# A fused attention and gMLP kernel on one core: a written-down job order, masks on TensorE, remainders in threes, and 19 DMA-transposed blocks

## The chip, the core and the metric

The kernel runs on one core of a Trainium2 chip. A core has five instruction queues: TensorE (PE, matmuls into the accumulator memory PSUM), VectorE (DVE), ScalarE (ACT), GpSimd (POOL) and SyncE (SP), which here does nothing but issue DMAs. The metric is the time of one execution on the device, in microseconds. PSUM has eight banks of 512 float32 values per partition.

## The reference

Input `x` has 2048 tokens of width 448. Two residual steps follow each other.

```
h  = x + Attn(layernorm(x))          # qkv = x @ wqkv, 16 heads of 28
h2 = h + Gmlp(layernorm(h))

Attn: token t looks at t, t-2, ..., t-14 (8 keys, those below 0 masked); softmax; @ wo
Gmlp: z = gelu(x @ w_in)             # 448 -> 1792, halves z1, z2
      g = w_sp @ layernorm(z2) + b_sp  # 2048 x 2048 over the tokens
      (z1 * g) @ w_out               # 896 -> 448
```

All inputs are bfloat16.

## The kernel before

**The attention.** The queries are cut into 18 blocks (`QN`: one of 128, nine of 112, eight of 114); a block's keys are its own tokens and the 14 before. Tokens are normalised in tiles of 128 (`stats`, `rstd_group`, `norm_transpose`) and transposed into `xhT`, on TensorE for the first eight tiles and by DMA after that. `qk_tile` makes 32 tiles of q or k of 512 tokens (four matmuls, one copy each), `v1_block` the values of a block. `scores` computes a block's 16 heads in 16 small matmuls on 28 of the 128 rows, ACT takes the exponential (L696), DVE multiplies it with a 0/1 mask (L700, three `Eslot` buffers), and `o_block` does 16 matmuls (L712) whose 29th column is the softmax's denominator; DVE divides (L720, L721). The result is transposed: by DMA where the block's length is a multiple of 16 (L726), else by TensorE with a copy out of PSUM (L729). `y_block` multiplies with `wo`, DVE adds the residual into `x_tm` (L743) and takes the statistics of the second layernorm.

**The gMLP.** The 448 input rows are three chunks of 128 and a remainder of 64. `packed` takes two accumulations at a time: six chunk matmuls of the first, the remainders of both (each pair on rows 0-63 and 64-127 of the array, L817), six chunk matmuls of the second (L811). There are 16 z2 blocks and 14 z1 tiles. Then 28 `g_tile`s (16 matmuls each, L874) alternate by token quarter with `wout_block`s (L898). In the last four blocks the residual enters PSUM through a matmul with the identity (L901); else DVE adds it.

**The order of the work.** Every operation is a job with a priority, a cost and the engines that can take it. `Sched.order` plays the jobs through once at build time: at each moment each free engine takes the ready job of the lowest priority number. What comes out is a fixed sequence for every queue, with semaphore waits between queues; on the chip an instruction that waits holds up all behind it on its queue. Banks 0-3 belong to the scores until the last block's scores have been placed. Warm-up matmuls (L573) have the priority 1e8, so they fill gaps. The mask is built by POOL and DVE at the start (L537 to L567, priorities -1000 and -300), the mixer's first matmuls depend on the load of the Gelu table (`r_gelu`), which depends on the last exponential.

## Time and profile before

| | |
|---|---|
| timed runs | 255.34, 255.38, 254.61 us (median 255.34) |
| the profiled execution | 254.57 us |
| its span, first to last instruction | 252.8 us |
| PE, DVE, ACT, POOL busy | 97%, 56%, 37%, 20% of the span |
| granted TensorE clock, mean | 0.993 |
| attention and lead-in / z2 and z1 / g and w_out | to about 82 / 82 to 131 / 131 to 249.8 us |

The time of an execution is longer than its span, since starting and ending it lie around the span. Views give an instruction's start from the span's start, its engine, its line and what it writes and reads. The chain of work that ended last is followed back from the last instruction: each piece was released by the one before, so what stands in it set the time. Matmuls overlap: the length of one (352 ns for 448 columns) is longer than the step from one to the next (189 ns), so costs on PE are read from starts.

### The profile page before, as it was taken

Reading aid. Unit: us, or ns where it says so; the run is one execution under the profiler, and the core shown is the slowest. Engines: PE = TensorE matmul, PEld = TensorE weight load, DVE = VectorE, ACT = ScalarE, POOL = GpSimd, SP = SyncE. Lnnn points to the kernel's source line nnn. Section 1 sums busy time; section 2 is a strip of 40 time slices with the busy share of each in tenths; the row PEclk is TensorE's granted clock in tenths of the full one; section 3 lists DMA queues with packets and bytes.
Section 4 is the critical chain, followed back from the end, with each engine's and each line's share of the span. In section 5 each row is a group of like instructions: output and inputs, shape, how many; then the busy total and the mean of one; then the engine's idle time right before and its main releaser. Section 6 shows DMA issues by size and latency. Waiting matters only on the chain.

```text
span 252.8 us, 4276 instructions
## 1 busy us (share of the span) xinstructions
PE 244.7 (97%) x1760; PEld 120.7 (48%) x1760; DVE 142.8 (56%) x303; ACT 93.3 (37%) x125; POOL 51.4 (20%) x85
## 2 busy tenths in 40 slices
PE   5799999999999999999999999999999999999995
PEld 1455555554555545444444444444444444444472
DVE  6798878789999888986203223423334332252240
ACT  2578787778599546666660000000000000000002
POOL 8305700002908480993000000000000000000000
PEclk9799999999999999999999999999999999999999
DMA  5931558956445591399999000020000100010002
GB/s 161 278 105 25 106 86 204 212 116 138 100 86 66 94 243 23 82 149 197 182 192 144 15 0 0 0 75 0 0 0 26 49 0 0 3 56 18 0 3 73
DMA packets 57060, 20.90 MB, mean 83 GB/s; under 512 B 50064, under 2 KB 56400, under 8 KB 57040
## 3 DMA queue, kind: packets, MB, share of 16 engines
q1 hardware_dynamic: 57040, 20.62, 39.2%
q8 instruction: 14, 0.23, 0.4%
q14 instruction: 6, 0.05, 0.1%
HBM read 6.60 MB, written 1.84 MB: 33 GB/s over the span
## 4 chain that ended last, share of the span: by engine, by line
PE 89%; ACT 4%; DVE 4%; DMA 1%; issue 0%
PE psum L874 38%; PE psum L811 15%; PE psum L657 10%; PE psum L898 8%; PE psum L670 5%; PE psum L740 3%; PE psum L817 3%; ACT regE L696 3%; PE psum L712 2%; PE psum L688 2%; ACT regW L582 1%; PE psum L639 1%; PE psum L573 1%; DVE ij L563 1%; DMA x_tm<-in_A_x_dram 1%; DVE x_tm L743 1%
## 5 line engine op out<-in xcount | busy, mean ns | idle before, releaser
L885 DVE TENSOR_TENSOR regE<-psum,regE 128x512 bf16<-128x512 f32 (+1 forms) x29 | 19.5, 674 | 76.3 <-PE psum L874 76.3
L874 PE MATMUL psum<-regW,regZ 128*128 128x512 bf16 (+1 forms) x240 | 48.9, 365 | 0.0
L874 PE MATMUL psum<-wspT_lo,regZ 128*128 128x512 bf16 x224 | 48.7, 379 | 0.0
L582 ACT ACTIVATE tring<-psum 128x448 bf16<-128x448 f32 x3 | 1.6, 545 | 116.4 <-PE psum L898 116.4
L874 PEld LDWEIGHTS psum<-regW,regZ 128*128 128x128 bf16 x240 | 23.4, 98 | 25.1
L874 PEld LDWEIGHTS psum<-wspT_lo,regZ 128*128 128x128 bf16 x224 | 21.9, 98 | 26.4
L657 PE MATMUL psum<-xhT,regZ 128*128 128x512 bf16 x128 | 31.1, 379 | 0.0
L696 ACT ACTIVATE regE<-psum 126x1792 bf16<-126x1792 f32 (+2 forms) x18 | 30.4, 1686 | 1.6 <-PE psum L688 1.5
L626 POOL TENSOR_SCALAR tring<-x_tm,ngm,rst 128x448 bf16<-128x448 bf16 (+1 forms) x32 | 24.5, 780 | 7.6 <-ACT rst L615 4.4
L898 PE MATMUL psum<-regE,regQ 128*128 128x448 bf16 x112 | 22.3, 352 | 0.0
L700 DVE TENSOR_TENSOR regE<-regE,maskb 126x1792 bf16<-126x1792 bf16 (+2 forms) x18 | 20.2, 1120 | 0.0
L811 PE MATMUL psum<-w_in,xhT 128*128 128x448 bf16 x96 | 19.5, 353 | 0.0
L593 DVE BATCH_NORM_STATS2 st<-x_tm 128x6 f32<-128x448 bf16 x32 | 18.6, 609 | 1.1 <-DMA x_tm<-in_A_x_dram 1.1
L811 PE MATMUL psum<-xhT,w_in 128*128 128x512 bf16 x84 | 19.0, 380 | 0.0
L670 PE MATMUL psum<-regW,xhT 128*128 128x448 bf16 (+1 forms) x72 | 17.2, 368 | 0.5 <-ACT rsy L613 0.5
L832 DVE BATCH_NORM_STATS2 st<-regZ 128x6 f32<-128x448 bf16 x32 | 17.5, 603 | 0.0
L657 PEld LDWEIGHTS psum<-xhT,regZ 128*128 128x128 bf16 x128 | 11.4, 97 | 11.9
L827 ACT ACTIVATE regZ<-psum 128x896 bf16<-128x896 f32 x16 | 14.0, 917 | 8.2 <-PE psum L817 6.1
L862 ACT ACTIVATE regQ<-psum 128x1024 bf16<-128x1024 f32 x14 | 13.7, 1023 | 8.4 <-PE psum L817 7.2
L582 ACT ACTIVATE regQ<-psum 128x512 bf16<-128x512 f32 x22 | 13.1, 597 | 8.8 <-PE psum L657 8.6
L898 PEld LDWEIGHTS psum<-regE,regQ 128*128 128x128 bf16 x112 | 11.0, 98 | 10.3
L582 ACT ACTIVATE regW<-psum 128x448 bf16<-128x448 f32 (+2 forms) x23 | 12.4, 551 | 7.3 <-PE psum L670 4.4
(70 smaller groups left out, 227.7 us busy)
## 6 DMA issues: line engine op xcount, KB each, us to landing
out_dram<-tring SPq DMA_DIRECT2D x16, 112.0 KB, 1.7
x_tm<-in_A_x_dram SPq DMA_DIRECT2D x3, 448.0 KB, 4.4
w_in<-in_B_w_in_dram SPq DMA_DIRECT2D x1, 1344.0 KB, 9.3
regE<-in_B_w_out_dram SPq DMA_DIRECT2D x1, 784.0 KB, 4.7
regW<-in_A_wqkv_dram SPq DMA_DIRECT2D x1, 672.0 KB, 5.7
regE<-in_B_b_sp_dram SPq DMA_DIRECT2D x1, 512.0 KB, 5.7
w_in<-in_B_w_in_dram SPq DMA_DIRECT2D x2, 224.0 KB, 9.3
regW<-in_A_wqkv_dram SPq DMA_DIRECT2D x1, 336.0 KB, 3.4
```

What stands on the lines that cost most here:

```text
L582: ways["act"] = (c, [lambda e: e.activation(dst(), src(), AF.Copy)])
L593: dve(prio, 0.62, lambda e: e.bn_stats(lnst[i][:, m, :], x_tm[:, m, :]), [r_x[m]], [r_stat[i][m]])
L626: job(prio, {"pool": (cp, [lambda e, c0=c0, c1=c1, s0=s0: e.tensor_scalar(tring[:, t.slot, c0:c1], x_tm[:, m, s0:s0 + c1 - c0], ngm[i][:, ...
L657: fns = [lambda e, c=c: e.matmul(bankcols(b, 512), wsrc[:, c, gg, :], xhT[:, c, col0:col0 + 512], start=(c == 0), stop=(c == NCH - 1)) for ...
L670: fns = [lambda e, c=c: e.matmul(bankcols(k, D)[0:nk], xhT[:, c, k0:k0 + nk], stg[:, c, 2 * D:3 * D], start=(c == 0), stop=(c == NCH - 1)) ...
L696: ej = job(prio + 1, {"act": (1.70, [lambda e: e.activation(Eheads(b), psum[0:nk, 0:2048].rearrange("p (h c) -> p h c", c=128)[:, :, 0:nq] ...
L700: dve(prio + 10, 1.12, lambda e: e.tensor_tensor(Eheads(b), Eheads(b), maskb[0:nk, mi:mi + 1, 0:nq].to_broadcast([nk, NHEAD, nq]), ALU.mul ...
L811: return [lambda e, i=i, c=c: e.matmul(out(i), lhs(i, c, slice(0, 128)), rhs(i, c, slice(0, 128)), start=(first and c == 0), stop=(not fir ...
L832: dve(prio + 2, 0.62, lambda e, i=i: e.bn_stats(st3[:, m, i, :], z2p[:, m, D * i:D * (i + 1)]), [r_z2p[m]], [r_stat[2][m]])
L874: fns = [lambda e, s=s: e.matmul(bankcols(k, n), z2p[:, s, fc * 128:(fc + 1) * 128], wsrc[:, s, coff:coff + n], start=(s == 0), stop=(s == ...
L885: dve(prio + 10, 0.70 * n / 512, lambda e: e.tensor_tensor(ub[:, u.slot, 0:n], bankcols(k, n), bb[:, t0:t0 + n], ALU.add), [k, r_bb], [u])
L898: fns = [lambda e, fc=fc: e.matmul(bankcols(k, D), z1p[:, fc, 128 * m:128 * m + 128], w_out[:, fc, :], start=(fc == 0 and not last), stop= ...
```

## The change

- **Order.** A list, `PLAN`, gives each of the 803 jobs its rank as its priority, and `ENGINE` ties 51 jobs to an engine. `Sched.order` still plays the jobs through, with other costs and latencies.
- **Blocks.** 19 blocks: 128, fourteen of 112, three of 96, one of 64. All are multiples of 16, so each output is transposed by DMA.
- **Masks.** For blocks 14 and 16 four matmuls of the identity with `maskn` (0 or -1e9) write PSUM first and the scores are added to that; DVE's multiplication is left out for these two.
- **Mask building.** The POOL work on it, and other fills, wait for the q/k weights; the DVE part has a later priority. The fill of `V1` with ones is cut to the one column that needs it.
- **Loads.** `x` block 1 is loaded ahead of the v weights.
- **q and k.** A `qk_tile` makes q and k together: eight matmuls into two banks and one copy of both.
- **Statistics.** For the first eight tiles of the second layernorm the final step (`bn_aggr`) is replaced by seven small POOL instructions (`aggregate`).
- **Remainders.** `packed` takes three accumulations, over z2 and z1 alike (30 in ten chains), and these depend on the last scores instead of the Gelu table.
- **The end.** The identity matmul is gone and DVE adds the residual in all blocks; block 15 is done in two halves of 224 columns, each with its own store.
- **Others.** 14 warm-up matmuls instead of 20; eight instead of nine w_sp blocks are loaded during the attention.

Counting jobs in the order in which they are made turns the list into names. TensorE begins: 7 warm-ups, transposes of tile 0, warm-up, tile 1, warm-up, v0, v1, warm-up, tile 2, warm-up, tile 3, warm-up, v2, q/k of tokens 0-511 (group 1, 0, 3), v3, warm-up, q/k group 2, warm-up, tiles 7, 5, scores 0, tiles 6, 4. The attention ends with: v17, scores 16, outputs 13, 15, y9, scores 17, output 16, y10, scores 18, first chunk of z2 block 0. The remainder jobs stand apart from each other, and three z1 tiles come ahead of z2 block 6. On DVE the order of the start is: statistics of tiles 0 and 1, normalise 0 and 1, statistics 3 and 2, copy of v0, normalise 2 and 3, first mask instruction, copy of tile 2, regrouping of a quarter of the q/k weights, the next mask instructions. SP issues: x0, x1, v weights, x2-3, the rest of v, q/k weights; later x transposes 8-11, w_sp 0, output 0, w_in, w_sp 1, x transposes 12-15, then outputs, w_sp blocks and transposes of h in turn.

```diff
-NWARM = 20
+NWARM = 14
+AGH = (0, 1)
+XPE = 2
+NLO = 8
+XONE = -99.7
+MKP = -100
+CHAIN = 3
+ADDMASK = (14, 16)
-QN = [128] + [112] * 9 + [NQ] * 8
+QN = [128] + [112] * 14 + [96] * 3 + [64]
+PLAN = (
+    15, 2, 21, 3, 1, 19, 0, 6, 4, 20, 44, 7, 18, 50, 5, 26, 57, 48, 8, 58, 16, 17, 54, 9, 59, 65, 60, 45, 61, 56,
...
-    LAT = {"pe": 0.20, "act": 0.10, "dve": 0.10, "pool": 0.15, "sp": 0.0}
+    LAT = {"pe": 0.12, "act": 0.06, "dve": 0.06, "pool": 0.08, "sp": 0.0}
...
-        load_x(-99, 1, 2)
-        load_x(-98.5, 2, 4)
+        load_x(XONE, 1, 2)
+        load_x(X23, 2, 4)
...
-        pool(2.2, lambda e: e.memset(V1, 1.0), writes=[r_Vones])
+        pool(0.2, lambda e: e.memset(V1[:, :, :, DH:DH + 1], 1.0), writes=[r_Vones])
+        pool(0.3, lambda e: e.iota(ij[:], [[1, 128]], base=0, channel_multiplier=1), r_stgqk[:1], [r_ij])
...
-        dve(-300, 0.2, lambda e: e.tensor_single_scalar(ij[:], ij[:], 1, ALU.bitwise_and), reads=[r_ij], writes=[r_ij])
+        dve(MKP, 0.2, lambda e: e.tensor_single_scalar(ij[:], ij[:], 1, ALU.bitwise_and), reads=[r_ij], writes=[r_ij])
...
+            dve(MKP + 1, 0.25, lambda e: e.tensor_scalar(maskn[:, 0, :], maskb[:, 0, 0:NQ], 1.0, MASKED, ALU.subtract, ALU.mult),
+                reads=[r_mask], writes=[r_maskn])
...
+        def aggregate(prio, i, lo, hi):
+            me, se, mo, so = (lnst[i][:, lo:hi, k] for k in (1, 2, 4, 5))
+            N, Y, T = (b_[i][:, lo:hi] for b_ in (ngm, rsy, rst))
...
+            p(lambda e: e.tensor_tensor(Y, me, mo, ALU.subtract), rs, [rc])
+            p(lambda e: e.tensor_tensor(N, me, mo, ALU.add), rs, r_ngm[i][lo:hi])
+            p(lambda e: e.tensor_tensor(Y, Y, Y, ALU.mult), [rc], [rc])
+            p(lambda e: e.tensor_tensor(T, se, so, ALU.add), rs, r_rstd[i][lo:hi])
+            p(lambda e: e.tensor_scalar(N, N, -0.5, 0.0, ALU.mult, ALU.add), r_ngm[i][lo:hi], r_ngm[i][lo:hi])
+            p(lambda e: e.tensor_scalar(T, T, 4.0 / D, 4.0 * EPS, ALU.mult, ALU.add), r_rstd[i][lo:hi], r_rstd[i][lo:hi])
+            p(lambda e: e.tensor_tensor(Y, Y, T, ALU.add), [rc] + r_rstd[i][lo:hi], [rc])
...
+        def qk_tile(prio, tc, gg):
...
+            b = Buf("qk%d_%d" % (tc, gg), p_bank, 2)
+            fns = [lambda e, i=i, w=w, c=c: e.matmul(bankcols(b, 512, i), w[:, c, gg, :], xhT[:, c, col0:col0 + 512],
+                                                     start=(c == 0), stop=(c == NCH - 1))
+                   for i, w in enumerate((wqp, wkp)) for c in range(NCH)]
+            copy(prio + 1, (1.22, 1.02), lambda: qkT[:, :, gg, col0:col0 + 512],
...
+            if b in ADDMASK:
+                add = [lambda e, hh=hh: e.matmul(
+                    psum[0:nk, hh * 512:hh * 512 + 512].rearrange("p (g c) -> p g c", c=128)[:, :, 0:nq],
+                    ident[0:nk, 0:nk], maskn[0:nk, 0:1, 0:nq].to_broadcast([nk, 4, nq]),
+                    start=True, stop=False, skip_group_check=True) for hh in range(4)]
+                fns = add + fns
...
-            one, two = jobs_
+            one, more = jobs_[0], jobs_[1:]
             turn = Buf("turn", p_turn)
+            job(one[0], {"pe": (cost(6, one), chunks(one, True))}, one[5], [one[1], turn])
+            fns = rest(one, True)
+            for p in more:
+                fns += rest(p, False)
...
+            parts = ((0, D // 2), (D // 2, D)) if m == NB - 1 else ((0, D),)
...
-                if last and n == 0:
-                    fns.insert(0, lambda e: e.matmul(bankcols(k, D), ident[:], x_tm[:, m, :], start=True, stop=False))
...
+        for rank, n in enumerate(PLAN):
+            sch.jobs[n].prio = rank
+        for eng, ns in ENGINE.items():
+            for n in ns:
+                sch.jobs[n].ways = {eng: sch.jobs[n].ways[eng]}
         sch.order()
```

More of the change, by code (lines that the diff above doesn't have):

```diff
@@ L242, in order @@
                     left[f] -= 1
-                    f.ready = max(f.ready, vis)
+                    f.ready = max(f.ready, end if set(f.ways) == {e} and not j.dma else vis)
                     if not left[f]:
@@ new lines, in wout_block @@
+            for h, (k, (c0, c1)) in enumerate(zip(ks, parts)):
+                t = Buf("out%d_%d" % (m, c0), p_tr)
+                dve(prio + 6 + h, 0.15 + 0.00106 * (c1 - c0), lambda e, k=k, t=t, c0=c0, c1=c1: e.tensor_tensor(
+                    tring[:, t.slot, c0:c1], bankcols(k, c1 - c0), x_tm[:, m, c0:c1], ALU.add), [k, r_x[m]], [t])
+                dma(prio + 7 + h, 112, lambda e, t=t, c0=c0, c1=c1: e.dma_start(OUT[128 * m:128 * m + 128, c0:c1], tring[:, t.slot, c0:c1]), [t], []).store = True
```

310 lines of the change are left out of this document (172 added, 138 removed), and 35 rows, old and new, of the table PLAN.

## The prediction

> **What bounds the kernel now.** I read the page first: TensorE (PE) is busy 97% of 252.8 us, so the question is which parts of that are work. The table of stretches answers it.
>
> ```profile
> 0.00:7.00 7.00, 3.52 (x8) 1.01 (x8) 4.83 (x9) 1.78 (x3) 6.36 (x20) 1.00 0.64 179
> 7.00:15.00 8.00, 7.40 (x40) 4.18 (x41) 6.00 (x20) 5.13 (x13) 1.70 (x5) 0.79 0.90 273
> ...
> 23.50:62.00 38.50, 38.50 (x508) 21.08 (x501) 31.85 (x57) 30.56 (x35) 7.38 (x9) 1.00 0.73 141
> 62.00:70.00 8.00, 7.97 (x86) 4.26 (x85) 7.81 (x18) 4.98 (x8) 6.18 (x9) 1.00 0.48 100
> 70.00:82.00 12.00, 11.01 (x180) 6.55 (x179) 11.65 (x24) 11.90 (x16) 5.70 (x8) 1.00 0.48 79
> ...
> 131.00:249.80 118.80, 118.77 (x581) 56.50 (x579) 39.08 (x70) 2.30 (x4) 0.00 (x0) 1.00 0.12 25
> ```
>
> Columns after the length: PE, weight loads, VectorE (DVE), ScalarE (ACT), GpSimd (POOL), the granted clock, DMA. From 15 us on PE is full except in 70 to 82, where ACT (11.90 of 12) and DVE (11.65) are full instead. The chain that ended last tells the same.
>
> ```profile
> 3.77 2.20 DVE ij L563
> ...
> 5.99 0.48 DVE pf L564
> ...
> 6.50 0.46 DVE pf L565
> ...
> 13.67 1.51 PE psum L670 x8
> 15.19 6.91 PE psum L657 x32
> ...
> 64.75 1.36 DVE regE L700
> ...
> 71.47 1.69 ACT regE L696
> 73.16 0.88 ACT regW L582 x2
> 74.04 1.58 ACT regE L696
> ```
>
> So three stretches do not belong to PE: the lead-in, where mask building (L563 to L565) holds DVE and with it the first normalisation; 62 to 68, where DVE owns the chain; and 71.5 to 81.3, where exponentials and PSUM copies on ACT do. All else is a stream of matmuls, and any matmul added or removed there moves the end by its own length.
>
> **The sum's base.** The profiled execution took 254.57 us, 1.77 more than its span and 0.3% under the median of the three timed runs (255.34; they lie between 254.61 and 255.38). Changes are added to 254.57. About 0.3% is also what a measurement of this kernel can tell from no change.
>
> **Lead-in.** Today block 0 is ready at 3.76 (its mean and variance), ACT's rsqrt ends at 4.33, but the normalisation runs only at 6.64, behind L563 (2.28 us) and its two followers; the first transposes start at 7.13, the first q/k tile at 15.02, by when PE has done four v blocks and four groups of transposes. In the changed order DVE goes from block 0's statistics to block 1's, then normalises: 3.76, plus 0.61 and 0.18 for block 1, plus 0.43, is about 5.0. What then gates the first q/k tile is the q/k weights (landed at 9.14 and 9.73), their regrouping (0.39 on DVE, 0.94 on ACT) and the copy of x block 3, which ACT has behind that regrouping: 9.73 + 0.94 + 0.60 is about 11.3; I take 11.4. The written order puts three v blocks before it, not four (0.80 each), so the gain is 15.02 - 11.4 - 0.80 = 2.8 us. Bounds: 3.4, if ACT's copy comes first; 1.6, if the first mask instruction, now just ahead of the copy of x block 2 on DVE, takes 2.28 again. Why did it take that?
>
> ```profile
> L563 DVE TENSOR_SCALAR ij<-ij 128x128 int32<-128x128 int32 x1 | 2.3, 2276 | 0.0
> L559 POOL MEMSET regW<- 128x2560 bf16 x1 | 2.2, 2231 | 0.0
> ```
>
> In the timeline L559 runs from 3.65 to 5.88 and L563 from 3.68 to 5.96: it ends as the memset does. The change shrinks the memset to one column in 32, and POOL's instructions beside the moved mask work take 0.24 to 0.39. [...]
>
> Warm-up matmuls go from 20 to 14. Two sit after the first q/k tiles (0.43 each), as two do today (22.60, 64.17): no difference. If the clock stays low longer (v blocks at 8.43 ran at half pace, 1.65 per four matmuls), that lies in the wait for the weights.
>
> **PE work.** Durations are starts of one job to the next, from the chain. Removed: eight groups of output transposes (L729, 0.20 to 0.21: 1.65) and four identity matmuls of the last four blocks (L901, 0.19: 0.76). Added: a nineteenth block, v 0.80 + scores 0.37 + output 0.39 = 1.56. Score jobs of 112 queries take 0.37, those of 114 take 0.31; eight of the latter go, eight x 0.06 = 0.48. The mask matmuls are four per block, of 448 and 384 columns. No row has this form; the nearest, full-height matmuls of 448 columns (L901), pace at 0.19, so 0.76 + 0.65 = 1.41; bounds 1.2 (in an open PE gap) and 1.8. Remainders (L817): today nine runs, each costing some 95 ns extra on the way in and again on the way out (a chunk before a remainder takes 285 or 311 instead of 189 or 216). The written order has ten separate runs of six: +0.2; bounds -0.9 (runs merge in pairs) and +0.2. In all -2.41 + 3.65, +1.2 us; bounds -0.1 and +1.6.
>
> **DVE, ACT and the stall.** From 71.45 to 82.50 PE did three v blocks, four transposes, five y blocks, three score and four output jobs, 9.4 us of work in 11.05: 1.7 waited. With 0.2 before 68.03, 1.9. The change takes from ACT eight copies of transposed output (0.56: -4.5) and about 1.9 in x copies, and adds a copy or so of net 1.2 (q/k copies go from 22 x 0.60 to 14 x 1.02, the price of a two-bank pass from L862), 0.9 of regrouping and 0.17 for one more exponential: about -4. From DVE it takes two masks (-2.2), eight aggregations (-1.4) and q/k copies (10 x 0.69 to two of at most 1.38: -4.1), and adds 0.85 (nineteenth block), 0.6 (v copy), 1.3 (x copies): about -5. Scores can also start some 5 us sooner, as first q/k tiles do, giving ACT that much more room, and the mixer's first matmuls wait only for the last scores. So I take the 1.9 as gone. What is late next is DVE: between the first q/k tile and the last scores it keeps some 60 us (15 masks 16, 17 divisions 15, 10 residual adds 6, 21 statistics 15, copies and normalisations 8) against 64 us of PE work, in a fixed order where each output job waits for its mask. A strict order on five queues will wait somewhere; the nearest row is today's own 1.9, and I take half of it, +1.0, bounds 0 and +4. Moving aggregation to POOL (seven instructions at 0.2 to 0.34, twice) puts about 2 us into the rsqrt of eight blocks; y and mixer work cover it. If that cover is gone, ACT's Ln waits with the next exponential behind it, 2 us each.
>
> **DMA.** Nine more output transposes ride SP's queue: 1.26 of queue time, 2.7 to landing, instead of 0.21 + 0.56 through PE and ACT. The y blocks that read them come some jobs later; cost nil while the queue keeps up (first rival). x block 1 goes ahead of the v weights by one 112 KB load: stgv landed at 4.65, xhT for the first v block is ready near 6, so it hides.
>
> **Tail.** The last block's copy took 0.62 after the last matmul; half a block (256 columns from PSUM took 0.42) saves 0.2. The extra store issue (0.33) lies under the second half's matmuls; bounds -0.3 and +0.3. After the last g tile (243.55) six matmuls (1.13) instead of seven cover its add and product on DVE, which ended 1.02 later: just hidden.
>
> **Sum:** -2.8 + 1.2 - 1.9 + 1.0 - 0.2 = -2.7; 254.57 - 2.7 = 251.9 us.
>
> **Rivals.** (1) SP's queue becomes the bound, slower. Between 22.8 and 82.0 it issued 33 transposes and three loads, 51.1 us busy of 59.2.
>
> ```profile
> 40.40 0.60 SPq L513 DMA_DIRECT2D w_in<-in_B_w_in_dram  x1
> 41.05 3.14 SPq L726 DMA_TRANSPOSE regW<-otm  x2
> 44.23 5.23 SPq L926 DMA_TRANSPOSE wspT_lo<-in_B_w_sp_dram  x1
> 49.50 2.57 SPq L726 DMA_TRANSPOSE regW<-otm  x2
> ```
>
> After the w_in load it stood for 5 us. Nine more transposes at 1.31 less one w_sp transpose are +10.2 against 8.1 free, in a window some 5 us shorter: 7 short. If none of it can go out later, outputs and normalised h land 7 late, y blocks and the mixer starve, and PE has nothing else: 251.9 - 1.0 + 7 = 258. It decides from about 3.7 us of such waiting on. Against it: four h transposes (5.1) are not needed until the mixer's second chain. Chance 0.15. (2) The stall only moves: DVE, near full, with two more long chains of POOL instructions beside it (a mask took 1.36 in the chain, 1.09 alone) keeps PE waiting as long as today or a little more: 1.9 to 2.6 in place of 1.0, 252.8 to 253.6, and with the lead-in's lower bound 254.8. [...] Chance 0.25. (3) The order fits so well that nothing new waits and the lead-in reaches 3.4: 251.9 - 1.0 - 0.6 - 0.3 = 250.0. Chance 0.15. The forecast itself, 250.6 to 253.2, has 0.45.
>
> **How the numbers follow.** The likeliest is 251.9. The range takes in the third rival with remainders merged (249.4) and reaches up to 255.6, which leaves out most of the first rival and a little below: under 2 in 10. Faster by over 0.3% means under 254.57: the forecast, the third rival and most of the second, 0.76; within 0.3%, the second's end and the start of the first, 0.09; slower 0.15.
>
> **What would show it.** First transposes near 5 and first q/k tile near 11.4; the first integer mask instruction well under 1 us; no transposes of outputs on PE; four 448-column matmuls of 0.19 ahead of two score jobs; ten remainder runs; mixer matmuls before the table load; PE's dense stretch from g to the last w_out shorter by 0.76 us; a last DVE piece near 0.4. The prediction is wrong if output jobs, y blocks or the first mixer chain wait more than 3 us in all, which the wait list would put down to DVE masks, to SP's transposes or to ACT's Ln, or if the first q/k tile starts after 13.

## The result, and the profile after

| | before | after |
|---|---|---|
| timed runs, median | 255.32 us (254.61 to 255.38, 4 runs) | 252.22 us (251.57 to 252.46, 4 runs) |
| profiled execution | 254.57 us | 252.46 us |
| its span | 252.8 us | 250.7 us |

The ratio is 0.9881, with a 95% interval of 0.9855 to 0.9907: the change makes the kernel 1.2% faster. The forecast was 251.9, in a range of 249.4 to 255.6. The sum was made for the profiled execution, where it foresaw 2.7 us less; there it is 2.11 less. Three of the four runs of the kernel before took about 255.3 here; in the experiments below it took over 255.0 in 16 of 48 runs and 254.4 to 254.9 in the rest. Against 254.6 the gain is 2.4 us, or 0.9%.

The table of stretches of the kernel after (columns as before: PE, weight loads, DVE, ACT, POOL, granted clock, DMA):

```profile
0.00:7.00 7.00, 4.55 (x18) 1.61 (x19) 4.22 (x10) 3.47 (x7) 2.51 (x13) 1.00 0.66 163
7.00:15.00 8.00, 6.79 (x36) 3.29 (x38) 5.74 (x17) 5.16 (x10) 4.11 (x11) 1.00 0.85 256
...
62.00:70.00 8.00, 7.84 (x110) 4.87 (x110) 7.46 (x14) 5.38 (x6) 6.06 (x8) 1.00 0.39 81
70.00:82.00 12.00, 11.71 (x189) 7.37 (x190) 10.27 (x22) 10.34 (x12) 5.55 (x15) 1.00 0.46 94
```

In 70 to 82 PE is busy for 11.71 us (11.01 before), while ACT fell from 11.90 to 10.34 and DVE from 11.65 to 10.27: neither is full there any more. (Some matmul records of this trace are missing, so PE's sums are a little low.) The chain that ended last, of the kernel after:

```profile
3.93 6.42 DMA regW<-in_A_wqkv_dram
...
10.43 0.95 ACT regZ L616
11.38 0.49 ACT xhT L663
11.88 0.14 issue
12.02 2.10 PE psum L762 x9
...
17.39 1.03 ACT regQ L663
18.42 0.05 issue
18.47 1.91 PE psum L762 x8
20.39 0.02 issue
20.41 1.03 ACT regQ L663
...
77.46 1.46 ACT regE L813
```

The mask building is gone from it. The lead-in is now a load (the q/k weights, landed at 10.35), their regrouping on ACT, the copy of x tile 3 behind that on the same engine, and the first q/k tile at 12.02. From there to the last matmul only three pieces do not belong to PE: two copies of q/k tiles (17.39 and 20.41) and one exponential (77.46).

To see where the 2.1 us come from, I cut each trace at the starts of certain matmuls. One v block (0.76) moved from before the first q/k tile to after it and is counted on the side where it was before.

| stretch | before | after | difference | foreseen |
|---|---|---|---|---|
| start to first q/k tile | 15.02 | 12.02 + 0.76 | -2.24 | -2.8 |
| first q/k tile to first g | 115.90 | 118.14 - 0.76 | +1.48 | +1.06 |
| first g to last matmul | 118.84 | 118.10 | -0.74 | -0.76 |
| last matmul to end of span | 3.06 | 2.47 | -0.59 | -0.2 |

Foreseen in the second row: PE work +1.2 without the identity matmuls' -0.76 that belong to the third row, the stall's -1.9 and the new waits' +1.0. So the attention as a whole became longer, and the gain lies at the two ends of the kernel. The experiments ask which parts of the change that is owed to.

### The profile page after: what moved, and what is told of

The parts are those of the page before. It is cut to its first block, busy times and chain, and to the rows that moved or that the text cites. A ratio compares the mean times of both kernels' runs of the same rounds, so it can differ in the third digit from the quotient of the medians.

```text
span 250.7 us, 4263 instructions
## 1 busy us (share of the span) xinstructions
PE 242.2 (97%) x1746; PEld 121.7 (49%) x1769; DVE 143.4 (57%) x296; ACT 90.8 (36%) x105; POOL 48.7 (19%) x97
## 4 chain that ended last, share of the span: by engine, by line
PE 92%; DMA 3%; ACT 2%; SPq 1%; issue 1%; DVE 0%; ACTq 0%
PE psum L1006 38%; PE psum L940 15%; PE psum L762 11%; PE psum L1031 8%; PE psum L779 5%; PE psum L860 5%; PE psum L832 3%; PE psum L946 3%; PE psum L797 3%; DMA regW<-in_A_wqkv_dram 3%; ACT regQ L663 1%; PE psum L747 1%; ACT regE L813 1%; PE psum L804 1%; SPq L565 1%
## 5 line engine op out<-in xcount | busy, mean ns | idle before, releaser
L1006 PEld LDWEIGHTS psum<-regW,regZ 128*128 128x128 bf16 x240 | 23.5, 98 | 25.0
L813 ACT ACTIVATE regE<-psum 126x1792 bf16<-126x1792 f32 (+3 forms) x19 | 30.5, 1605 | 6.4 <-PE psum L797 5.0
L762 PE MATMUL psum<-xhT,regZ 128*128 128x512 bf16 x118 | 28.1, 379 | 1.4 <-issue 0.5
L734 POOL TENSOR_SCALAR tring<-x_tm,ngm,rst 128x448 bf16<-128x448 bf16 (+1 forms) x32 | 21.3, 678 | 7.1 <-ACT rst L717 4.7
L1031 PE MATMUL psum<-regE,regQ 128*128 128x448 bf16 (+1 forms) x119 | 21.9, 341 | 0.0
L966 DVE BATCH_NORM_STATS2 st<-regZ 128x6 f32<-128x448 bf16 x32 | 19.1, 610 | 4.1 <-ACT regZ L961 3.7
L820 DVE TENSOR_TENSOR regE<-regE,maskb 126x1792 bf16<-126x1792 bf16 (+3 forms) x17 | 18.1, 1063 | 2.7 <-ACT regE L813 2.5
L779 PE MATMUL psum<-regW,xhT 128*126 128x448 bf16 (+3 forms) x76 | 17.1, 357 | 1.4 <-DVE xhT L665 0.7
L663 ACT ACTIVATE regQ<-psum 128x1024 bf16<-128x1024 f32 x14 | 14.3, 1023 | 7.4 <-PE psum L762 7.2
L990 ACT ACTIVATE regQ<-psum 128x1024 bf16<-128x1024 f32 x14 | 14.3, 1023 | 6.6 <-PE psum L940 4.5
L1037 DVE TENSOR_TENSOR tring<-psum,x_tm 128x448 bf16<-128x448 f32 (+1 forms) x17 | 10.1, 597 | 8.8 <-PE psum L1031 8.5
L860 PE MATMUL psum<-regW 128*128 128x448 bf16 x64 | 13.9, 352 | 0.0
```

The source lines that it names most:

```text
L734: job(prio, {"pool": (cp, [lambda e, c0=c0, c1=c1, s0=s0: e.tensor_scalar(tring[:, t.slot, c0:c1], x_tm[:, m, s0:s0 + c1 - c0], ngm[i][:, ...
L762: fns = [lambda e, i=i, w=w, c=c: e.matmul(bankcols(b, 512, i), w[:, c, gg, :], xhT[:, c, col0:col0 + 512], start=(c == 0), stop=(c == NCH ...
L779: fns = [lambda e, c=c: e.matmul(bankcols(k, D)[0:nk], xhT[:, c, k0:k0 + nk], stg[:, c, 2 * D:3 * D], start=(c == 0), stop=(c == NCH - 1)) ...
L813: ej = job(prio + 1, {"act": (0.17 + 0.0133 * nq, [lambda e: e.activation(Eheads(b), psum[0:nk, 0:2048].rearrange("p (h c) -> p h c", c=12 ...
L820: job(prio + MP, {by: (cost, [lambda e: e.tensor_tensor(Eheads(b), Eheads(b), maskb[0:nk, mi:mi + 1, 0:nq].to_broadcast([nk, NHEAD, nq]), ...
L860: fns = [lambda e, c=c: e.matmul(bankcols(k, D), OT[:, c, 128 * m:128 * m + 128], wo_sb[:, c, :], start=(c == 0), stop=(c == NCH - 1)) for ...
```

## The experiments

Runs called "b" are the kernel before with one part of the change; runs called "a" are the changed kernel with one part undone or altered. The ratio is to the kernel before, run on the same chip: its median was 255.32 beside the changed kernel and 254.58 to 254.64 beside all others, so medians of two runs that differ by a few tenths are not told apart here. All starts below are from the profiled execution of each run, which need not be the median one (a_noplan 255.69, b_leadin 261.14, a_spfree 258.74).

| run | median us | ratio, 95% | first q/k (v blocks ahead) | q/k to g | g to last matmul | tail |
|---|---|---|---|---|---|---|
| before | 254.6 | | 15.02 (4) | 115.90 | 118.84 | 3.06 |
| after | 252.22 | 0.9855 to 0.9907 | 12.02 (3) | 118.14 | 118.10 | 2.47 |
| b_memset | 252.79 | 0.9894 to 0.9954 | 12.78 (4) | 115.89 | 118.84 | 3.05 |
| b_noident | 254.51 | 0.9966 to 0.9993 | 15.57 (4) | 115.89 | 118.08 | 3.17 |
| b_leadin | 259.70 | 1.0151 to 1.0242 | 15.82 (4) | 121.68 | 118.84 | 3.07 |
| b_best | 252.23 | 0.9880 to 0.9941 | 14.02 (4) | 115.89 | 118.10 | 2.64 |
| a_noplan | 257.03 (7 runs; an eighth took 259.85) | 1.0046 to 1.0095 | 13.58 (4) | 119.82 | 118.10 | 2.47 |
| a_dvemask | 252.89 | 0.9909 to 0.9942 | 11.75 (3) | 118.77 | 118.10 | 2.47 |
| a_x1late | 253.02 | 0.9921 to 0.9976 | 11.78 (3) | 118.67 | 118.10 | 2.47 |
| a_spfree | 256.89 | 1.0049 to 1.0096 | 11.88 (3) | 124.59 | 118.10 | 2.46 |
| a_spfix | 253.02 | 0.9912 to 0.9943 | 11.61 (3) | 118.91 | 118.10 | 2.47 |
| a_whole | 252.37 | 0.9883 to 0.9918 | 11.91 (3) | 118.13 | 118.08 | 2.83 |
| a_gate | 252.68 | 0.9902 to 0.9941 | 11.53 (3) | 118.91 | 118.10 | 2.47 |
| a_lead | 252.38 | 0.9894 to 0.9932 | 11.20 (3) | 118.82 | 118.10 | 2.47 |

The table shows how cleanly the kernel falls into parts: 118.10 or 118.84 from g on, to 0.02 us, depending only on the identity matmuls; and 115.89 for the old attention in four programs out of four.

### The fill alone (b_memset)

```
-        pool(2.2, lambda e: e.memset(V1, 1.0), writes=[r_Vones])
+        pool(2.2, lambda e: e.memset(V1[:, :, :, DH:DH + 1], 1.0), writes=[r_Vones])
```

The planner's cost is left at 2.2, so that the order of the work stays that of the kernel before.

> The kernel before, in its own order, except that the fill of V1 with ones (L559) writes one column in 32 instead of all: 80 elements per partition for 2560. Theory (the long fill is what holds the integer mask instruction): L563 falls from 2276 ns to under 500, the first normalisation runs at about 4.9 instead of 6.64, the first transposes near 5.3; the first q/k tile moves from 15.02 by 1 to 2 us, as the weights and tile 3 then gate it, and the span goes from 252.8 to about 251.3. Rival (a 128x128 int32 instruction simply takes 2.3 us): L563 stays at 2.2 to 2.3 and nothing moves.

The ratio is 0.9924: this one line has the whole gain of the lead-in. Its first q/k tile starts at 12.78 with four v blocks ahead, exactly the changed kernel's 12.02 and one v block of 0.76. That the two agree so closely is chance: there the q/k weights gate the tile; here it is x block 1 (landed at 6.22), through the statistics, normalisations and transposes behind it and PE's own work from 9.61 on. From its groups of instructions:

```profile
L563 DVE TENSOR_SCALAR ij<-ij 128x128 int32<-128x128 int32 x1 | 0.9, 874 | 0.0
...
L559 POOL MEMSET regW<- 128x80 bf16 x1 | 0.4, 446 | 0.0
```

L563 took 2276 ns beside the long fill, and 874 beside the short one and the two instructions that follow it on POOL (together 0.8 us). Two other kernels complete the series. In b_leadin, where POOL has nothing beside it:

```profile
L563 DVE TENSOR_SCALAR ij<-ij 128x128 int32<-128x128 int32 x1 | 0.2, 194 | 0.0
```

and in the kernel after, beside short fills (L639; the L643 line is taken up below):

```profile
L643 DVE TENSOR_TENSOR maskb<-mf,pf 128x128 bf16<-128x128 f32 x1 | 1.0, 989 | 0.7 <-POOL mf L632 0.7
...
L639 DVE TENSOR_SCALAR ij<-ij 128x128 int32<-128x128 int32 x1 | 0.3, 303 | 0.9 <-POOL ij L626 0.9
```

One instruction, one tile, and 194, 303, 874 or 2276 ns by what POOL does meanwhile. The L643 line repeats it with another pair: 989 ns, while a POOL copy of 0.93 us started 0.09 us before it; in the kernel before the same instruction, with nothing beside it (at 9.23), took 0.26. The traces show that much, and not the cause.

The old stall in 70 to 82 is still there in this kernel, 2.24 us earlier with all the rest (PE 11.02 of 12; DVE 11.66 and ACT 11.90, as full as before):

```profile
67.76:79.76 12.00, 11.02 (x180) 6.54 (x179) 11.66 (x24) 11.90 (x16) 5.71 (x8) 1.00 0.60 79
```

There is a second difference between the two executions. From the timeline of PE in the kernel before, where PE stood from 4.89 to 7.13 and waited for the normalisation:

```profile
7.37 0.59 PE L573 MATMUL psum<-warm 128*128 128x512 bf16 x2
8.43 1.65 PE L670 MATMUL psum<-regW,xhT 128*128 128x448 bf16 x4 [0.47 <-ACT rsy L613]
...
12.05 0.97 PE L670 MATMUL psum<-regW,xhT 128*126 128x448 bf16 x4
```

and in b_memset:

```profile
5.93 0.59 PE L573 MATMUL psum<-warm 128*128 128x512 bf16 x2
6.99 0.92 PE L670 MATMUL psum<-regW,xhT 128*128 128x448 bf16 x4 [0.46 <-ACT xhT L582]
```

The same v block took 1.65 and 0.92. In the kernel before matmuls of 448 columns step at 373 ns from 8.43 on and at 189 from 12.05 on. The table of stretches of the kernel before, cut finer, has the granted clock as the third number from the end:

```profile
6.00:8.00 2.00, 0.83 (x6) 0.34 (x6) 1.93 (x6) 0.43 (x1) 1.77 (x8) 1.00 1.03 356
8.00:10.00 2.00, 1.57 (x5) 0.72 (x6) 1.78 (x7) 0.55 (x3) 0.14 (x1) 0.52 0.96 250
10.00:12.00 2.00, 2.00 (x13) 1.06 (x11) 0.85 (x3) 1.74 (x7) 0.79 (x1) 0.62 0.82 209
12.00:14.00 2.00, 2.00 (x16) 1.39 (x14) 1.41 (x4) 1.88 (x3) 0.00 (x0) 1.00 1.09 380
```

The lost 48% and 38% of two stretches of 2 us, 0.96 and 0.76 us, make about 3.4 us at half pace. Ahead of it PE had stood for 2.25 us in one piece (4.89 to 7.13) and had then done four transposes and two warm-up matmuls at full pace (0.40 and 0.59 us, as in b_memset). What set the half pace off is not shown; in b_leadin (below), too, it came after PE had stood, there for 2.30 us. So of the 2.24 us, a part is not work waiting for DVE but work done at half pace afterwards. How large it is stays open, as the pace differs between executions with the short fill too (b_best, below).

### The identity matmuls alone (b_noident)

```
-                                                 start=(fc == 0 and not last), stop=(fc == FC7 - 1)) for fc in fcs]
-                if last and n == 0:
-                    fns.insert(0, lambda e: e.matmul(bankcols(k, D), ident[:], x_tm[:, m, :], start=True, stop=False))
+                                                 start=(fc == 0), stop=(fc == FC7 - 1)) for fc in fcs]
...
-            if last:
-                copy(prio + 6, ...)
-            else:
+            if True:
                 dve(prio + 6, ...)
```

> The kernel before, with the residual of the last four blocks added by VectorE as in all others, so that the four identity matmuls are gone and nothing else in the order changes ahead of them. Theory (outside three stretches the end moves by the length of any matmul): faster by 4 x 0.19 = 0.76 us, the last matmul ending at 249.0 instead of 249.8, the tail as before (VectorE's add 0.62). Rival (the last products on VectorE then come late): the second part of block 12 waits for the last product, and 0.2 to 0.4 of the 0.76 is given back.

From g to the last matmul it is 118.08 against 118.84: -0.76, as worked out. The time moved by only 0.2%. In the profiled execution (254.53) the first q/k tile was 0.55 later than in the kernel before: from the first transposes at 7.13 on, its chain holds PE's work alone, at half pace until 12.2 at least (a v block took 1.65 us at 8.64 and 0.92 at 12.64). The ten times fall apart into four of 253.85 to 253.97 and six of 254.49 to 254.80, and the seventeen of the kernel before into twelve of 254.42 to 254.87 and five of 255.26 to 255.40. Group against group the gain is some 0.7; among the ten, the upper group is merely the larger one.

### The parts of the lead-in alone (b_leadin)

```
-        load_x(-99, 1, 2)
+        load_x(-99.7, 1, 2)
...
-        pool(0.3, lambda e: e.iota(ij[:], ...), writes=[r_ij])
+        pool(0.3, lambda e: e.iota(ij[:], ...), r_stgqk[:1], [r_ij])
...
-        dve(-300, 0.2, lambda e: e.tensor_single_scalar(ij[:], ij[:], 1, ALU.bitwise_and), reads=[r_ij], writes=[r_ij])
+        dve(-100, 0.2, lambda e: e.tensor_single_scalar(ij[:], ij[:], 1, ALU.bitwise_and), reads=[r_ij], writes=[r_ij])
```

and so for the other mask and fill instructions, with the short fill; the old planner plays the jobs through again.

> The kernel before with the changed kernel's lead-in alone: x block 1 loaded ahead of the v weights, POOL's mask work and fills behind the q/k weights, VectorE's mask work late, V1's fill cut to one column; the order is planned anew by the old priorities and costs. Theory (lead-in and attention add up): the first q/k tile starts 2 to 2.5 us earlier and the time falls by about as much, to a ratio of 0.991. Rival (the gain of the lead-in reaches the end only with an order made for it, since VectorE and ScalarE bound 62 to 82 us): first q/k tile as early, but the stretch from 60 to 85 waits longer and the ratio stays above 0.995.

It is 2% slower: more parts than b_memset, and 6.9 us worse. That the parts of the lead-in add up falls with it. From its table of stretches:

```profile
7.00:15.00 8.00, 4.96 (x24) 2.79 (x25) 5.94 (x16) 4.15 (x10) 3.08 (x10) 0.87 0.74 238
15.00:23.50 8.50, 8.50 (x44) 4.12 (x43) 5.20 (x19) 5.41 (x12) 0.00 (x0) 0.92 0.15 50
23.50:62.00 38.50, 36.08 (x437) 19.74 (x433) 27.20 (x52) 29.38 (x37) 7.68 (x10) 0.96 0.67 125
```

PE has nothing from 10.6 to 12.9 and then works at half pace again (eight matmuls of 448 columns took 3.18 us at 12.86 and 1.67 at 7.16); and the attention, which the planner laid out anew, holds 2.4 us of waits in 23.5 to 62 where the kernel before has none, at a granted clock of 0.96 there against 1.00. In all it takes 121.68 instead of 115.90, without any change to its work.

### The changed kernel without its written order (a_noplan)

```
-        for rank, n in enumerate(PLAN):
-            sch.jobs[n].prio = rank
-        for eng, ns in ENGINE.items():
-            for n in ns:
-                sch.jobs[n].ways = {eng: sch.jobs[n].ways[eng]}
```

> The changed kernel without the written ranks and the ties to engines: the same jobs, costs and latencies, planned by the priorities of the code. Theory (the written order is worth the waits in the attention, which I put at 1.9 less 1.0, and little else): slower than the changed kernel by 0.5 to 2.5 us, near 253.5, TensorE waiting between 60 and 85. Rival (the order is the larger part of the gain): 255 or more. Rival (order without effect, all of the gain is in the jobs): within 0.4 us of the changed kernel.

It is 0.7% slower than the kernel before; all the parts are in it, so without the list the change is a loss. By the profiled executions the list is worth 3.25 us of span (this one, 255.69, is among its three shortest; by the medians it is 4.8): 0.80 before the first q/k tile (13.58 against 12.78 with as many v blocks) and 2.44 from there to g. Its waits are easy to see in the table of stretches (PE lacks 1.35 and 1.52 us):

```profile
70.00:82.00 12.00, 10.65 (x210) 7.11 (x210) 10.46 (x21) 9.67 (x11) 8.39 (x17) 1.00 0.48 94
82.00:110.00 28.00, 26.48 (x170) 12.45 (x169) 23.90 (x59) 13.83 (x17) 12.69 (x20) 1.00 0.84 161
```

and PE's list of waits from 62 to 110 names them (us in total, times, longest):

```profile
PE psum L797 <- ACT regE L813: 1.4, 2, 1.1
PE psum L946 <- DVE x_tm L863: 0.8, 1, 0.8
PE psum L946 <- DVE mv L968: 0.7, 1, 0.7
```

### Three small edits to the kernel before (b_best)

The short fill, no identity matmuls, and the last block in two halves, with all else as before (the diffs are those of b_memset, b_noident and the change's own last block).

> The kernel before in its own order, with three edits alone: V1's fill cut to one column in 32, the residual of the last four blocks added by VectorE, block 15 in two halves. Theory (the three gains add: 1.9 from the fill, 0.76 from the identity matmuls, 0.3 to 0.6 from the tail): about 251.5 us, span about 249.4, faster than the changed kernel by some 0.7 us. Rival (the gains overlap, or the last product comes late on VectorE): 252.5 or more.

252.23 us over nine runs that lie between 251.00 and 254.52: with the intervals given, not to be told from the changed kernel. Its profiled execution explains why it is not at 249.4, which b_memset's lead-in would give (12.78 + 115.89 + 118.10 + 2.64 = 249.4 of span): it reached its first q/k tile at 14.02. Its PE timeline:

```profile
5.70 0.61 PE L639 MATMUL psum<-ident,tring 128*128 128x128 bf16 x4 [0.73 <-DVE tring L630]
6.10 1.06 PE L573 MATMUL psum<-warm 128*128 128x512 bf16 x2
7.20 1.65 PE L670 MATMUL psum<-regW,xhT 128*128 128x448 bf16 x4
```

Its instructions up to there are those of b_memset, and start at the same 5.70, but b_memset's PE was at full pace by then (0.40 us for these four transposes, 0.92 for the v block) and this one's stayed at half until 9.9. So the moment from which PE has its full pace lies over 4 us apart in these two executions; why is not shown. That the spread of the nine times comes from this is likely, but only the profiled execution shows its pace. Three of the nine lie at 251.00 to 251.21, about where a span of 249.4 would put them.

### Masks of two blocks back on DVE (a_dvemask)

```
-ADDMASK = (14, 16)
+ADDMASK = ()
```

with the two multiplications ranked right behind their exponentials and the ranks of all else kept. The planner still plays the jobs through, and made another order of TensorE's work between 72 and 88: the last three score jobs come earlier among the output and y jobs, and the first z2 chunk comes ahead of a y block.

> The changed kernel with the masks of blocks 14 and 16 back on VectorE (the eight mask matmuls are gone; each of the two multiplications is ranked right behind its exponential). Theory (a mask on TensorE costs TensorE its length, about 1.5 us for both, and what it saves on VectorE hides): faster by 1 to 1.5 us. Rival (VectorE is the bound at the end of the attention): the two multiplications of 1.08 and 0.95 come back as waits of output jobs 14 and 16, and the time is the same or up to 0.6 slower.

Not faster, 252.89, and 0.63 longer from the first q/k tile to g. In 70 to 80 PE's matmuls fell behind their steps by 3.61 us, in the changed kernel by 1.62: the 1.63 us of mask matmuls that are gone came back as 2.0 of waits. Its list of waits in that stretch:

```profile
PEld psum L799 <- ACT regE L815: 2.1, 3, 1.1
PE psum L799 <- ACT regE L815: 1.5, 3, 0.7
```

The scores wait for the exponentials to empty their banks, and ACT for the scores in turn (1.4 us in three waits). In this pair of kernels the masks on PE pay for themselves, by some 0.4 us in that stretch. Whether the waits come from the masks or from the scores' new places is not shown, since both changed at once.

### Block 1 of x loaded late again (a_x1late)

```
-        for rank, n in enumerate(PLAN):
+        plan = [n for n in PLAN if n not in (6, 7, 5)]
+        at = plan.index(4) + 1
+        plan = plan[:at] + [5, 6, 7] + plan[at:]
+        for rank, n in enumerate(plan):
```

> The changed kernel with the loads at the start in the old order: v weights, then x block 1, then x 2 and 3; the planner moves the jobs of the first 12 us along. Theory (x block 1 ahead of the v weights makes the q/k weights land later: 10.35, 10.52 and 11.06 in three kernels with it, 9.45 to 10.25 in three without): they land at 9.4 to 9.8, the first q/k tile comes 0.5 to 0.8 earlier, and the time falls by about as much. Rival (x block 1's own lateness, at 6 instead of 3.3, gates the v blocks): first q/k tile no earlier, the time the same or slower by 0.5.

The q/k weights landed at 9.58 instead of 10.35, but the first q/k tile moved by only 0.24, to 11.78: ACT now came to the copy of x tile 3 later (11.13 to 11.72). The rest is 0.53 longer: PE waits 0.54 ahead of a y block at 97.88, and the planner had changed the order of the statistics and of VectorE's and ScalarE's early work too. So 253.02 does not price the order of the loads by itself; the 0.24 of the lead-in, too, is from one execution. Over all fourteen traces, the last of the q/k weights landed between 9.34 and 11.06 (mean 10.20) in the nine with x block 1 ahead, and between 9.45 and 10.25 (mean 9.73) in the five without. In the seven of the nine that have the changed kernel's whole order of loads it is 9.34 to 10.35 (mean 10.03): 0.3 later, and less than these seven differ among themselves.

### SP's queue relieved (a_spfree, a_spfix)

The first rival was that SP's queue becomes the bound. The first attempt moves the eight w_sp transposes out of the attention and lets the planner play the list:

```
-        for rank, n in enumerate(PLAN):
+        late, his = list(range(630, 638)), [649, 650, 648]
+        plan = [n for n in PLAN if n not in late + his]
+        at = min(plan.index(n) for n in range(638, 646))
+        plan = plan[:at] + late + plan[at:]
...
+        for rank, n in enumerate(plan):
```

> The changed kernel with the eight w_sp transposes that run during the attention issued behind the last transposes of h instead, and three later w_sp blocks behind all of those; eight issues of 1.3 us leave SP's queue between 22 and 82 us. Theory (SP's queue is not the bound): the stretch to the first g tile stays within 0.4 us. Rival (it holds y blocks and the mixer up): that stretch shortens by 1 us or more. In both cases the last w_sp block may land after 130, and the first g tiles wait; that part is told apart by the time of the last z1 matmul.

It is 4.7 us slower than the changed kernel, and answers nothing: eight DMAs fewer made the planner choose otherwise on TensorE too (y blocks ahead of scores, the last output jobs after z2's first chunks). PE's waits from 78 to 92 were then:

```profile
PE psum L946 <- DVE otm L841: 1.7, 1, 1.7
PE psum L860 <- DMA regW<-otm: 1.7, 1, 1.7
```

So the second attempt writes down, for every queue, the sequence that the changed kernel has, and changes SP's alone:

```
-        for rank, n in enumerate(PLAN):
-            sch.jobs[n].prio = rank
+        jobs = list(sch.jobs)
+        for eng, ns in QUEUES.items():
+            for rank, n in enumerate(ns):
+                jobs[n].prio, jobs[n].ways = rank, {eng: jobs[n].ways[eng]}
+                if rank:
+                    jobs[n].deps.add(jobs[ns[rank - 1]])
```

> The eight w_sp transposes taken out of the attention again, but with TensorE, VectorE, ScalarE and GpSimd held to the changed kernel's own sequence, job by job; only SyncE's order differs. This separates the freed queue from the reordering that the first attempt caused. If SyncE's queue does not bound the attention (first rival of the prediction wrong), the first g tile stays at 130.2 within 0.3 and the time at 252.2 within 0.4. If output transposes were held up behind the w_sp ones, the wait before the last scores (0.46 near 78) and part of the other waits in 60 to 90 go, and the time falls by 0.5 or more. If the w_sp blocks are now late for g, g waits and the time rises.

From the first q/k tile to g it took 118.91, 0.77 more than the changed kernel. But a_gate and a_lead, which are held in the same way and keep the eight transposes where they were, took 118.91 and 118.82: the 0.77 belongs to the holding, and the relief of SP is worth 0.00. The last four outputs ahead of the transposes of h were issued at 74.5 to 78.5 instead of 76.9 to 81.5, and nobody was waiting for them. The first rival is wrong. What the holding costs is seen at one place. PE in a_gate:

```profile
83.00 0.56 PE L832 MATMUL psum<-regW,regE 110*128 110x29 bf16 x16
83.98 2.64 PE L860 MATMUL psum<-regW 128*128 128x448 bf16 x12 [0.42 <-DVE x_tm L863]
```

and in the kernel after:

```profile
83.50 0.56 PE L832 MATMUL psum<-regW,regE 110*128 110x29 bf16 x16
83.91 2.43 PE L860 MATMUL psum<-regW 128*128 128x448 bf16 x12
```

With the same instructions in the same order, the y blocks (L860) wait for the residual add (L863) of an earlier y block, 0.79 us in all. PSUM banks are given out as the planner plays the jobs through, and the held sequence, played with other start times, handed these blocks other banks. That this is the reason is argued from the wait's two ends, not tried. The comparison of a_spfix with a_gate stands on kernels that both have this wait.

### The last block whole (a_whole)

```
-            parts = ((0, D // 2), (D // 2, D)) if m == NB - 1 else ((0, D),)
+            parts = ((0, D),)
...
```

> The changed kernel with its last block in one piece again: one accumulation of 448 columns, one residual add, one store; everything before it in the same order. In the changed kernel the span ended 2.47 us after the last matmul, in the kernel before 3.05. If the halving is what shortened the tail by 0.58, the tail here is about 3.05 and the time 0.4 to 0.6 above the changed kernel's, about 252.7. If the tail was shortened by DVE's add in place of ACT's copy, or if it is the final store's landing that varies, the tail stays at 2.5 to 2.7 and the time within 0.2 of the changed kernel's.

The tail was 2.83: the halving is worth 0.36 of the 0.59. DVE's last piece in the kernel after, and in this one:

```profile
248.29 0.39 DVE L1037 TENSOR_TENSOR tring<-psum,x_tm 128x224 bf16<-128x224 f32 x1 [0.28 <-PE psum L1031]
```

```profile
248.16 0.62 DVE L1037 TENSOR_TENSOR tring<-psum,x_tm 128x448 bf16<-128x448 f32 x1 [0.70 <-PE psum L1031]
```

0.23 is the shorter piece, and 0.13 the smaller last store (1.53 from issue to landing instead of 1.66). The other 0.23 come from the order of the last two blocks. In the kernel before both finish together, and their stores are issued at 250.19 and 250.56, the second waiting for the first and taking 1.77; in a_whole they are 1.33 apart. The time, 252.37, can't be told from 252.22.

### What gates the first q/k tile (a_gate, a_lead)

Both hold all queues to the changed kernel's sequence (as in a_spfix) but for these moves:

```
 ScalarE: ... copy of v1 |
-  regroup k weights 0 | copy of x tile 3 | ...
+  copy of x tile 3 | regroup k weights 0 | ...
 VectorE: ... normalise 3 |
-  first mask instruction | copy of x tile 2 | regroup q weights 0 | ...
+  copy of x tile 2 | regroup q weights 0 | first mask instruction | ...
```

> The changed kernel with two swaps and all queues otherwise held to its sequence: ScalarE copies x tile 3 before it regroups the first k weights, and VectorE copies x tile 2 and regroups its weights before the first integer mask instruction (which waited for GpSimd's iota). First q/k tile: 12.02 less the 0.58 of the copy that stood behind the regrouping, about 11.45, the end of the regrouping. If the first q/k tile's start sets the end (as the prediction's sum took it), the time falls by the same 0.55, to 251.7. If instead the chain through VectorE's statistics, ScalarE's rsqrt and its copy of the fourth q/k tile (ending at 21.43) sets the first scores, these move by 0.25 at most and the time stays at 252.0 to 252.3.

The first q/k tile started at 11.53. All that follows it moved along: from there to the first scores it is 9.47 in both kernels. In a_spfix, a_whole, a_dvemask, a_x1late and a_spfree, whose first q/k tiles start between 11.61 and 11.91, it is 9.47 or 9.48 too. So its start does set what follows, as the sum had it, and the other reading falls. The gain itself can't be read from this execution, as its weights landed at 9.34, earlier than any other's; the copy of x tile 3, at 9.95, then held the regrouping up and not the weights. In a_lead they landed at 10.02 and the first q/k tile started 1.18 later; in the changed kernel, a_whole, a_spfix, a_dvemask and a_spfree it is 1.66 or 1.67 each time. By a_lead's one execution, the copy behind the regrouping costs 0.49.

a_lead adds to this:

```
-  q/k group 3 | v3 | warm-up | q/k group 2 | warm-up | transposes 7, 5 | scores 0
+  q/k group 3 | q/k group 2 | v3 | warm-ups | transposes 7, 5 | scores 0
```

and, on VectorE and ScalarE, the statistics, rsqrt and normalisation of tiles 4 to 7 ahead of the statistics of tiles 10, 15, 9 and 11.

> The two swaps of the former run, and the fourth q/k tile right after the third, v3 behind it; on VectorE the final statistics of tiles 5 and 6 and the normalisation of tiles 4 to 7 ahead of the statistics of tiles 10, 15, 9 and 11; ScalarE's rsqrt for tiles 4 to 7 ahead of its third q/k copy. TensorE waits that it should end: 0.37 before the first q/k tile, 0.31 + 0.51 + 0.32 and 0.27 between 17.9 and 23, with two warm-ups of 0.86 that then lie elsewhere. If that is right, the first scores start near 19.8 in place of 21.49, TensorE's end moves by 0.9 to 1.7 us and the time is 250.5 to 251.3. If the attention is bound by VectorE and ScalarE behind the first scores, more waits at 60 to 80 take it back and the time stays within 0.4 of 252.2; if the later statistics of tiles 8 to 11 delay their q/k tiles, it is slower than that.

The two swaps do what they were to do; the rest does not. Of the 0.82 by which the first q/k tile is earlier (11.20), 0.33 is the landing of the weights and 0.49 the swap. The first scores then start at 20.15 instead of 21.49, but the v block behind them at 21.37 instead of 22.28, 0.91 earlier, and the first z2 chunk, too, is 0.91 earlier: the further moves give 0.09. In the timeline of PE, the waits are now at the transposes around those scores and behind them:

```profile
19.29 0.92 PE L747 MATMUL psum<-ident,tring 128*128 128x128 bf16 x8
20.15 0.40 PE L797 MATMUL psum<-regQ 28*128 28x128 bf16 x16
20.48 0.62 PE L747 MATMUL psum<-ident,tring 128*128 128x128 bf16 x8
21.37 0.97 PE L779 MATMUL psum<-regW,xhT 128*126 128x448 bf16 x4 [0.26 <-DVE xhT L665]
```

Eight transposes are 0.43 us of work and take 0.86 and 0.88 here: DVE, which copies them, is busy with the statistics of tiles 10, 15, 9 and 11 until 20.0. At 83 the bank wait of the holding took 0.79 back, so the time is that of the changed kernel, 252.38. The swap of copy and regrouping without the holding would be worth 0.49 by these traces; that kernel was not run, and no run here clearly beats the changed kernel.

## Why the prediction was right, point by point

**Lead-in, -2.8; measured -2.24.** The chain of the sum is the chain of the trace: weights landed, regrouping 0.95, copy of x tile 3 behind it, first q/k tile 1.67 after the landing (11.4 against 9.73 in the sum, the same 1.67). The mis-sized term is the landing: 9.73 was taken from the kernel before, and it was 10.35. That x block 1 ahead "hides" did not hold: the sum had the v weights landed at 4.65 and looked at this load alone, but x tiles 2 and 3 went ahead of the second half of the v weights too. That half landed at 6.85, and PE waited 0.70 for it ahead of the first v block (6.94). It cost nothing here, since the q/k weights gate the first q/k tile. These land some 0.3 us later on average with this order of loads; what that is worth is within the spread. The 2.28 of the first mask instruction did not return (0.30). The other bound, ACT's copy first, was named 3.4 and is worth 0.49, not 0.6.

What the prediction did not see is how little of the change is needed for it: one shortened fill gives the same lead-in. Nor did it separate the half pace of the v blocks, which it mentioned but put into "the wait for the weights".

**PE work, +1.2.** -0.76 for the identity matmuls was right twice (0.76 in b_noident, 0.74 in the change). The mask matmuls came to 1.63 with what waited at their ends, against 1.41, within the bounds of 1.2 and 1.8. The ten remainder runs came as written.

**Stall, -1.9, and new waits, +1.0.** Together -0.9 was foreseen. Taking the work as foreseen, +1.24 + 0.76 = +2.0, and +1.48 as measured, it was -0.5. The stall of 70 to 82 did go, to one wait of 0.46 near 78, and ACT and DVE lost 1.4 to 1.6 us of busy time in that window, as the sum's reason has it. Which of the parts carries this is not shown: with the two masks back on DVE 2.0 us of waits return, but in another order of the scores (a_dvemask), and with the masks on PE and the planner's own order PE still lacks 1.35 us there (a_noplan). The new waits were not where they were expected, on DVE between scores and outputs, but at the start: between 17.9 and 23 PE waits 1.2 us, behind v3, for a free pair of banks, for the copy of the fourth q/k tile, and for the transposed tiles 4 to 7. a_lead, which moves those pieces, gets only 0.09 us out of them: the wait turns to DVE's copies of the transposed tiles, as it would if DVE bounded that stretch by its whole work and not by one late piece.

**DMA, nil.** Right for SP's queue: a_spfix.

**Tail, -0.2; measured -0.59.** The halving gives 0.36, since the last store shrinks too, and the rest comes from the last two stores no longer meeting, which the prediction did not look at.

**The rivals.** SP as the bound: wrong, by a_spfix. (Its 10.2 us of added issues should read 10.5, nine at 1.31 less one.) The stall only moves: half right, about 1.2 of the 1.9 turned up elsewhere, but earlier and not on DVE's long chains. POOL's 14 small instructions, the two chains that this rival set beside DVE, cost DVE nothing that shows: in the kernel after, four DVE instructions ran beside them and took 0.61, 1.09, 0.62 and 0.25 us; others of their kind, with no POOL instruction beside them, took up to 0.63, 1.09, 0.62 and 0.26. Where a mask met one of the 14, it was POOL's instruction that took longer, 1.15 us in place of 0.20:

```profile
59.03 1.15 POOL L698 TENSOR_TENSOR ngm<-st 128x4 f32<-128x4 f32 x1
59.03 1.09 DVE L820 TENSOR_TENSOR regE<-regE,maskb 126x1792 bf16<-126x1792 bf16 x1 [0.16 <-ACT regE L813]
```

All fits: wrong by those 1.2 us.

**What the whole comes to.** The sum was right in its sign and nearly in its size, with some luck: the 0.39 more at the tail, which the sum did not have, about makes up for the 0.42 more in the attention. And the gain is not where the effort went. From the first q/k tile to g the new attention takes 117.4 against the old one's 115.9. The written order makes good 3.25 us (by the profiled executions) of what the new parts lose without it, and the three edits of b_best, with the old attention, come to the same time.

## What to carry to other kernels

Before an order is rewritten by hand, take the long instructions out of the way of the first work: here a VectorE instruction took 2.28 us beside a fill of 2.23 on GpSimd and 0.87 with that fill shortened, and TensorE, which had stood for 2.25 us, ran some 3.4 us at half pace soon after. Try each part of a large change alone, with all queues held as they were; a planner that plays the jobs again can move the time by 2% with no change to the work, and an experiment that lets it do so does not test its one edit. Even the holding cost 0.77 us here. Where a load gates the start, take its landing from several executions and not from one, and look at whether the times of a kernel fall into groups before a small difference of medians is read.

## What the runs showed of the hardware

- One VectorE instruction (128x128 int32) took 194, 303, 874 or 2276 ns, by what GpSimd ran beside it; another (128x128, float32 to bfloat16) 0.26 or 0.99.
- TensorE did not have its full pace from the start: in the kernel after, a warm-up matmul took 0.63 us at 4.19 and 0.38 from 5.19 on, in b_memset the pace was full from 5.70 on, in b_best it was half until 9.9 and in b_noident until 12.2 or later. It was half again from 8.4 to 11.5 in the kernel before, after it had stood from 4.9 to 7.1, and from 12.9 to 16.3 in b_leadin, after it had stood from 10.6 to 12.9. In b_best the granted clock shows 1.00 for its half-pace stretch; the steps between matmuls (373 against 189 ns for 448 columns) show the pace.
- The same load, behind the same loads of the queue, landed up to 1.0 us apart in seven executions (9.34 to 10.35).
- When a VectorE mask (1.09 us) and a small GpSimd instruction started together at 59.03, the GpSimd one took 1.15 us in place of 0.20 and the mask its usual time.
